# Three chained layers on one core: value products by pairs of query blocks, projections and output products at fixed steps

## The chip, the cores and the metric

The kernel runs on one core of a Trainium2 chip. The metric is the device time of one execution in microseconds (us), as the median of several. TensorE (PE in the profile) multiplies matrices, VectorE (DVE) and ScalarE (ACT) work on vectors and empty PSUM, where products land, GpSimd (POOL) works on vectors in SBUF, and SyncE (SP) issues most transfers. Each engine works through a queue of its own in order; semaphores hold an instruction until what it needs is there.

## The reference, cut to what matters

Three layers follow each other on 4 batches of 544 rows (32 global and 512 local ones) of width 512.

```python
out_l = sm(where(|i - j| <= 32, q k^T / 8) with 32 global keys) v       # 8 heads of 64, local and global rows
x = rows of all heads side by side                                       # [4, 544, 512]

for e in range(4):                                                       # second layer: 4 experts, each one causal head
    q, k, v = x @ wq[e], x @ wk[e], x @ wv[e]
    a = softmax(where(j > i, -1e9, q @ k^T / 8))
    out += gate[e] * (a @ v @ wo[e])                                     # gate: top 2 of 4

xk = mu_k * x + (1 - mu_k) * x_prev                                      # third layer, x_prev: the row before
xr = mu_r * x + (1 - mu_r) * x_prev
result = sigmoid(xr @ w_r) * (relu(xk @ w_k) ** 2 @ w_v)
```

## The kernel before, in words

The text calls the three layers A, C and D. The projections that feed C are called B; they run inside A and C.

**A** (step `n`, the loop at L813) computes local attention for 16 pairs of heads and leaves its result transposed in SBUF, one tile `xT[b]` a batch (channels on partitions, 544 rows along the free dimension). From `n` = 16 to 32 the loop at L861 spreads the 15 projection groups of batch 0 over its steps. The steps of C begin at `n` = 33, while A still ends.

**B** (`b_groups`, L624) is 15 groups a batch, in this order: `b_split` of the first half (256 rows; `xT` into a high and a low part, ACT L385 and POOL L386), value products of blocks 0 and 1 (`b_v`, 12 products each), q and k of the first pair of experts, q and k of the second pair (`b_qk`, 12 products each); then the same for the second half (288 rows), with the gating `b_gate` behind the value products. Every product with a weight is three (`mm3`, L93: high by high, high by low, low by high).

**C** (`c_step(m)`, L759) goes over 36 units, 9 a batch: query blocks 0 to 2 of the first pair of experts, the rows of the last 32 of the batch ("l"), block 3, and blocks 0 to 3 of the second pair. Step `m` holds these parts, in this order of the code:

- the scores of unit `m` (`c_qk`: PE L102, DVE L504, ACT L506);
- the norm of unit `m-1` (`c_norm`: DVE L517 to L519, POOL L522);
- some groups of the list `fill`: of B for batch b+1, and of the output products of batch b-1 (`e_wo`, 8 groups of 6 products, evicted by ACT L622);
- the transposes of unit `m-2` (`c_tp`: PE L531 into PSUM, evictions to the tile `cpt` by ACT L534 for one expert and DVE L536 for the other);
- the value products of unit `m-3` (`c_pv`: PE L602, each block alone; PSUM is emptied into `ytH` and `ytL` by ACT L612 and DVE L613 when block 2 and when block 3 are done);
- at `m` = 32 (`MIX`) the mixing of the first rows for D (`d_mix(0)`: ACT L675 and L679, DVE L676, POOL L680), and at `m` = 33 to 36 the first four products `d_k` of D;
- in two of three steps a job of the list `jobs` (L808): load 128 rows of a weight of D (21 loads, the first of them `wo`), and the split of the load before into high and low parts (`split_wd`, L137: ACT L144, L145, L159, POOL L147, L160, DVE L149, L150, L151, the first of each engine queued behind the engine's last score, norm or A instruction by `after`).

`fill` gets 15 groups when a batch begins and, at its fourth step, the 8 output groups in front of them; the number taken at a step follows from what is left (L774 to L776):

```python
k = -(-len(fill) // max(1, 9 - it)) if not (it < 3 and b > 0) else 2
if it in (3, 4, 5, 6) and b > 0:
    k = max(k, 3)
```

The order of this code is a wish, not the order of the queues. The build (`schedule_with_timeline_sim=True`, L975) plays all instructions through a simulated timeline and queues on each engine what is ready there first, the earlier in the code where two are ready. `after(ins)` (`tc.issue_after`) forbids an instruction to be queued ahead of `ins` on its engine; it makes nothing wait for `ins` to end.

**D** (the loop at L883) takes the 2176 rows in 9 blocks: `d_k`, `d_v` and `d_r` on PE with `d_mix` of the next block beside them.

Buffers that matter here: PSUM tag "a" with 6 tiles (scores, transposes, projections, output products, `d_k`), PSUM tag "x" with 2 (`y` of `c_pv`), `cpt` 2, `x` (the split) 1, `y` 2, `vC` 2, `qk` 3.

Of the kernel before, what the change touches and what calls it, by code (L numbers as in the profile page):

```python
# [18 lines left out]
S = SL + SG  # L19
# [10 lines left out]
MIX, K0, FIRST = 32, 33, 4  # L30
# [15 lines left out]
def chain_kernel(ctx: ExitStack, tc: tile.TileContext, kq, vw, vgd, w_gate, wq, wk, wv, wo,  # L46
# [526 lines left out]
    def l_tp(b):  # L573
        t = pl
        o = T("ptl", [5, 128], f"ptl{b}")
        pT = ps_t(f"lT{b}")
# [10 lines left out]
    yps, yHL = {}, {}  # L587

    def c_pv(b, ep, i):
        if ep == 0 and i == 0:  # L590
            yHL[b] = [T("y", [2, S], f"yt{s}{b}", F32R) for s in "HL"]
        if i in (0, NB - 1):
            yps[b, ep] = ps_x(f"y{b}{ep}{i}")
        yp = yps[b, ep]
        pt = cpt.pop((b, ep, i))
        lastq = i == NB - 1
        n = 160 if lastq else 128
        o0 = 0 if lastq else i * 128
        for j in range(i + 1):
            for e in ((0, 1), (1, 0))[j % 2]:  # L600
                hh = 2 * ep + e
                nc.tensor.matmul(yp[64 * e:64 * e + 64, o0:o0 + n], vC[b][:, j, hh * HD:(hh + 1) * HD],  # L602
                                 pt[:, e, j, 0:n], start=j == 0, stop=j == i and not lastq)
        if lastq:
# [4 lines left out]
        if i >= NB - 2:  # L609
            yH, yL = yHL[b]  # L610
            cc, src = (slice(384, S), yp[:, :160]) if lastq else (slice(0, 384), yp[:, :384])
            nc.scalar.copy(yH[:, ep, cc], src)  # L612
            nc.vector.tensor_sub(yL[:, ep, cc], src, v32(yH[:, ep, cc]))  # L613

    def e_wo(b, c, half):
        yH, yL = yHL[b]
        cc = slice(half * HALF, (half + 1) * HALF)
        p = ps_t(f"po{b}{c}{half}")
        for ep in range(2):
            mm3(p[:, :HALF], woS[0][:, ep, c * 128:(c + 1) * 128], woS[1][:, ep, c * 128:(c + 1) * 128],  # L620
                yH[:, ep, cc], yL[:, ep, cc], ep == 0, ep == 1)
        nc.scalar.copy(xT[b][:, c, 1 + half * HALF:1 + (half + 1) * HALF], p[:, :HALF])  # L622

    def b_groups(b):  # L624
        gs = []
# [11 lines left out]
    def wo_groups(b):  # L637
        return [lambda c=c, half=half: e_wo(b, c, half) for c in range(NC) for half in range(2)]
# [120 lines left out]
    def c_step(m):  # L759
        nonlocal fill, pending  # L760
        if m < NCU:
            b, it = divmod(m, 9)
            u = units[m]
            l_qk(b) if u[1] == "l" else c_qk(*u)
        else:
            b, it = B, m - NCU
        if it == 0 and b + 1 < B:
            fill += b_groups(b + 1)
        if it == 3 and 0 < b:
            fill = wo_groups(b - 1) + fill  # L770
# [3 lines left out]
        k = -(-len(fill) // max(1, 9 - it)) if not (it < 3 and b > 0) else 2  # L774
        if it in (3, 4, 5, 6) and b > 0:
            k = max(k, 3)  # L776
        for g in fill[:k]:
            g()
        del fill[:k]
# [3 lines left out]
        if 0 <= m - 3 < NCU:  # L783
            u = units[m - 3]
            if u[1] != "l":
                c_pv(*u)
# [192 lines left out]
```

## Time and profile before

| | us |
|---|---|
| median of 3 runs | 567.74 (565.76 to 572.1) |
| the profiled execution | 568.83 |
| its span, first to last instruction | 567.0 |
| of it PE busy | 544.6 |

The profiled execution has 1.8 us outside its span. In the rows below an instruction stands as engine, line of the kernel, operation, the tile that it writes <- the tiles that it reads, and its form (partitions times columns); "po" are the output products, "pv" and "pb" the projections, "C" the scores, "cT" the transposes, "y" the value products of C. Time in brackets is idle time of the engine just before, with what ended it. The rows that carry the argument stand below the change.

### The profile page before, as it was taken

What the parts mean: (1) busy time and instruction counts of PE and PEld (TensorE: products, weight loads), DVE (VectorE), ACT (ScalarE), POOL (GpSimd) and SP (SyncE); (2) the same over time, 40 slices, a digit from 0 to 9 for tenths busy, and PEclk for the clock granted to TensorE, in tenths of its full rate; (3) what the DMA queues carried; (4) which work ended last, traced back from release to release, by engine and by line L of the source; (5) the groups of instructions that cost most, each with busy time, mean ns of one, the idle gap of its engine ahead of it and who ended that gap; (6) DMA issues with size and microseconds to landing.
All of it is one profiled execution on the core that took longest, in us unless ns stands there. A gap on an engine that the chain in (4) does not pass through costs nothing.

```text
span 567.0 us, 12852 instructions
## 1 busy us (share of the span) xinstructions
PE 544.6 (96%) x4670; PEld 458.4 (81%) x4670; DVE 326.5 (58%) x1129; ACT 337.0 (59%) x1019; POOL 312.7 (55%) x416
## 2 busy tenths in 40 slices
PE   6899999999898999999987999999999999999997
PEld 3576777788787888788776798989898989898895
DVE  3677765664888779668999656442534252324211
ACT  5789765674667586668688468454545453534221
POOL 3578744453568786959688765443434343335120
PEclk9799999999998999899998999999999999999999
DMA  8998433020143442432740220000000010100000
GB/s 326 278 315 249 162 124 125 3 95 1 39 132 129 136 144 94 150 113 76 297 145 5 76 75 15 25 20 18 21 19 32 7 38 2 39 1 37 1 20 37
DMA packets 24383, 51.31 MB, mean 90 GB/s; under 512 B 10112, under 2 KB 11136, under 8 KB 23680
## 3 DMA queue, kind: packets, MB, share of 16 engines
q1 hardware_dynamic: 23744, 50.08, 26.1%
q8 instruction: 37, 0.61, 0.4%
q10 hardware_dynamic: 576, 0.41, 0.2%
q14 instruction: 26, 0.21, 0.1%
HBM read 39.74 MB, written 10.75 MB: 89 GB/s over the span
## 4 chain that ended last, share of the span: by engine, by line
PE 77%; DVE 13%; ACT 4%; POOL 3%; DMA 2%; issue 1%; SPq 0%; ACTq 0%; DVEq 0%; POOLq 0%
PE v L94 5%; PE v L95 5%; PE v L96 5%; PE k L96 5%; PE k L95 5%; PE k L94 5%; PE S L230 4%; PE y L602 3%; PE r L95 3%; PE r L94 3%; PE r L96 3%; PE x L348 3%; PE pT L280 2%; PE C L102 2%; PE cT L531 2%; PE po L94 2%
## 5 line engine op out<-in xcount | busy, mean ns | idle before, releaser
L696 POOL TENSOR_TENSOR kk<-k2r,kk 128x256 fp32r<-128x256 f32 x64 | 48.5, 761 | 83.6 <-ACT kk L695 83.6
L693 DVE TENSOR_TENSOR k2r<-ksr 128x256 f32<-128x256 f32 x64 | 30.6, 477 | 88.2 <-ACT ksr L692 84.6
L522 POOL TENSOR_TENSOR csm<-csm,crc 128x128 f32<-128x128 f32 (+3 forms) x64 | 52.7, 845 | 28.7 <-DVE crc L519 16.6
L243 ACT ACTIVATE sm<-sm,mn 128x160 f32<-128x160 f32 x128 | 53.4, 418 | 22.1 <-DVE mn L240 21.8
L676 DVE SCALAR_TENSOR_TENSOR mmr<-xT,mu,mtr 128x256 f32<-128x256 f32 (+4 forms) x96 | 53.9, 599 | 16.6 <-POOL m0L L680 5.7
L692 ACT ACTIVATE ksr<-k 128x256 f32<-128x256 f32 x64 | 24.1, 377 | 49.3 <-PE k L96 49.2
L261 POOL TENSOR_TENSOR pn<-sm,rc 128x256 f32<-128x256 f32 x64 | 37.9, 613 | 22.7 <-PE pT L280 14.0
L680 POOL TENSOR_TENSOR m1L<-mmr,m1H 128x256 fp32r<-128x256 f32 (+1 forms) x36 | 26.3, 744 | 42.4 <-ACT m1H L679 38.0
L506 ACT ACTIVATE csm<-csm,cmn 128x128 f32<-128x128 f32 (+3 forms) x64 | 35.8, 561 | 19.8 <-DVE cmn L504 14.3
L675 ACT ACTIVATE mtr<-xT,omu 128x256 f32<-128x256 f32 (+4 forms) x96 | 39.7, 441 | 6.8 <-DVE mmr L676 6.6
L695 ACT CAST kk<-k2r 128x256 fp32r<-128x256 f32 x64 | 25.8, 404 | 27.1 <-DVE k2r L693 25.4
L230 PE MATMUL S<-kq 64*64 64x160 f32 x512 | 33.1, 327 | 5.9 <-DMA kq<-in_kq_dram 3.9
L240 DVE CUSTOM_DVE_ANT_0 sm<-S,band 128x160 f32<-128x160 f32 x128 | 33.9, 316 | 5.4 <-PE S L230 5.0
L602 PE MATMUL y<-cpt,vC 128*64 128x128 f32 (+1 forms) x320 | 31.6, 299 | 2.8 <-ACT cpt L534 2.7
L741 DVE TENSOR_TENSOR o<-v,rt 128x512 f32<-128x512 f32 x17 | 11.6, 686 | 36.4 <-ACT m1H L679 21.8
L504 DVE CUSTOM_DVE_ANT_0 csm<-C,causal 128x128 f32<-128x128 f32 (+3 forms) x64 | 29.7, 483 | 4.7 <-PE C L102 4.5
L230 PEld LDWEIGHTS S<-kq 64*64 64x64 f32 x512 | 20.7, 141 | 13.7 <-DMA kq<-in_kq_dram 3.9
L102 PE MATMUL C<-qk 64*128 64x128 f32 (+3 forms) x192 | 29.2, 359 | 0.1
L602 PEld LDWEIGHTS y<-cpt,vC 128*64 128x64 f32 x320 | 20.1, 138 | 10.6 <-issue 4.1
L679 ACT CAST m1H<-mmr 128x256 fp32r<-128x256 f32 (+1 forms) x36 | 13.4, 391 | 25.5 <-DVE mmr L676 13.1
L386 POOL TENSOR_TENSOR x<-xT,x 128x256 fp32r<-128x256 f32 (+1 forms) x32 | 24.2, 784 | 7.8 <-ACT x L385 4.1
L348 PE MATMUL x<-pt,vw 128*64 128x64 f32 x512 | 28.4, 233 | 0.0
(407 smaller groups left out, 1913.5 us busy)
## 6 DMA issues: line engine op xcount, KB each, us to landing
kq<-in_kq_dram SPq DMA_DIRECT2D x15, 688.0 KB, 5.5
vw<-in_vw_dram SPq DMA_DIRECT2D x16, 512.0 KB, 5.4
out_dram<-o SPq DMA_DIRECT2D x17, 256.0 KB, 2.0
wrawv<-in_moe_w_v_dram SPq DMA_DIRECT2D x8, 512.0 KB, 3.6
wrawk<-in_moe_w_k_dram SPq DMA_DIRECT2D x8, 512.0 KB, 3.6
wrawr<-in_moe_w_r_dram SPq DMA_DIRECT2D x4, 512.0 KB, 3.6
dv0H<-wgv SPq DMA_DIRECT2D x4, 256.0 KB, 2.9
dv0L<-wyv SPq DMA_DIRECT2D x4, 256.0 KB, 2.4
```

The source lines that it names most:

```text
L94: nc.tensor.matmul(o, wH, xH, start=start, stop=False)
L95: nc.tensor.matmul(o, wH, xL, start=False, stop=False)
L96: nc.tensor.matmul(o, wL, xH, start=False, stop=stop)
L102: nc.tensor.matmul(op[0], op[a], op[x], start=n == 0, stop=n == 2)
L230: nc.tensor.matmul(st[h][64 * c:64 * c + 64, i * W:(i + 1) * W], t[rr, 64 * blk:64 * blk + 64], t[rr, KT0 + 96 * blk:KT0 + 96 * blk + W], ...
L243: last_act = nc.scalar.activation(ts[:, h, i], ts[:, h, i], AF.Exp, bias=mn[:, c:c + 1], scale=-1.0, accum_out=su[:, c:c + 1])
L348: nc.tensor.matmul(xs[pp][rr, 64 * blk:64 * blk + 64], w, pt[2 * pp + m // 2][:, 2 * h + m % 2, 64 * c:64 * c + 64], start=blk == 0, stop= ...
L522: last_pool = nc.gpsimd.tensor_tensor(t[:, :w], t[:, :w], rc[:, e:e + 1].to_broadcast([128, w]), op=ALU.mult)
L602: nc.tensor.matmul(yp[64 * e:64 * e + 64, o0:o0 + n], vC[b][:, j, hh * HD:(hh + 1) * HD], pt[:, e, j, 0:n], start=j == 0, stop=j == i and ...
L675: nc.scalar.mul(mt[:, cc], xp, omu[:, kind, c:c + 1])
L676: nc.vector.scalar_tensor_tensor(mm[:, cc], x, mu[:, kind, c:c + 1], mt[:, cc], op0=ALU.mult, op1=ALU.add)
L696: nc.gpsimd.tensor_sub(hl[1], k2, v32(hl[0]))
```

## The change

- **Value products by pairs.** `c_pv` is called for odd blocks only and does blocks 2p and 2p+1 into one PSUM tile. It is emptied into `ytH` and `ytL` after each pair: 256 columns and 288 (before: 384 and 160). In the step it stands behind the norm and ahead of the projections, where before it stood behind the transposes.
- **Output kept apart by halves.** One pair of tiles `yH`, `yL` serves all batches; the output groups take its columns as 256 and 288 (before 272 and 272), and are given out by half.
- **Fixed steps.** The table `STEPS` says at which step of a batch each group runs; `plan_fill` makes the plan. The steps of batch b hold: 1: the first split of b+1, and four output groups (first half) of b-1; 2: values 0; 3: values 1, q; 4: k, one output group (second half); 5: q, k, the second split, one output group; 6: two output groups, values 2; 7: values 3, gating; 8: q, k; 9, which is step 0 of the next batch: the last q, k. Of batch 0, 13 groups stay in A and 2 go to step 0 of C. The first output groups of batch 3 stand at step 37, the second behind the last step.
- **First mixing.** `MIX` goes from 32 to 31, and its ACT and DVE instructions are queued behind the last eviction of `cpt` on their engines. `c_tp` now names its evictions as `last_act` and `last_dve`, so the weight splits of a step are queued behind them too.
- **Jobs** run in three of four steps (before two of three).
- **Last rows.** The 32 last rows of a batch are multiplied over all 128 partitions (before over the batch's own 32); the rest of the tile is zeroed by a POOL memset, one a batch.

```diff
-MIX, K0, FIRST = 32, 33, 4
+MIX, K0, FIRST = 31, 33, 4
...
     def c_tp(b, ep, i):
+        nonlocal last_act, last_dve
...
             if e == 0:
-                nc.scalar.copy(pt[:, e, 0:i + 1, 0:128], src)
+                last_act = nc.scalar.copy(pt[:, e, 0:i + 1, 0:128], src)
             else:
-                nc.vector.tensor_copy(pt[:, e, 0:i + 1, 0:128], src)
+                last_dve = nc.vector.tensor_copy(pt[:, e, 0:i + 1, 0:128], src)
...
         o = T("ptl", [5, 128], f"ptl{b}")
+        nc.gpsimd.memset(o[:, NB], 0.0)
...
+    yHL = []
+
+    def c_pv(b, ep, pr):
+
+        if not yHL:
+            yHL.extend(T("y", [2, S], f"yt{s}", F32R) for s in "HL")
+        yp = ps_x(f"y{b}{ep}{pr}")
+        for i in (2 * pr, 2 * pr + 1):
+            pt = cpt.pop((b, ep, i))
+            n = 160 if i == NB - 1 else 128
+            o0 = 128 * (i % 2)
+            for j in range(i + 1):
+                for e in ((0, 1), (1, 0))[j % 2]:
+                    hh = 2 * ep + e
+                    nc.tensor.matmul(yp[64 * e:64 * e + 64, o0:o0 + n], vC[b][:, j, hh * HD:(hh + 1) * HD],
+                                     pt[:, e, j, 0:n], start=j == 0, stop=j == i and i < NB - 1)
+        if pr == 1:
             for e in range(2):
                 hh = 2 * ep + e
-                nc.tensor.matmul(yp[64 * e:64 * e + 64, 128:160], v_last[SG * b:SG * b + SG, hh * HD:(hh + 1) * HD],
-                                 ptl[b][SG * b:SG * b + SG, NB, hh * 32:(hh + 1) * 32], start=False, stop=True)
...
+                nc.tensor.matmul(yp[64 * e:64 * e + 64, 256:288], v_last[:, hh * HD:(hh + 1) * HD],
+                                 ptl[b][:, NB, hh * 32:(hh + 1) * 32], start=False, stop=True)
+        yH, yL = yHL
+        cc, src = (slice(256, S), yp[:, :288]) if pr else (slice(0, 256), yp[:, :256])
+        nc.scalar.copy(yH[:, ep, cc], src)
+        nc.vector.tensor_sub(yL[:, ep, cc], src, v32(yH[:, ep, cc]))
...
+    STEPS = {1: [(0, 0), (1, 0, 0), (1, 0, 1), (1, 0, 2), (1, 0, 3)], 2: [(0, 1)], 3: [(0, 2), (0, 3)],
+             4: [(0, 4), (1, 1, 0)], 5: [(0, 5), (0, 6), (0, 7), (1, 1, 1)], 6: [(1, 1, 2), (1, 1, 3), (0, 8)],
+             7: [(0, 9), (0, 10)], 8: [(0, 11), (0, 12)], 9: [(0, 13), (0, 14)]}
...
+        gs = b_groups(0)
+        plan[0] = gs[13:]
...
+                    if op[0] == 0 and nxt:
+                        plan.setdefault(9 * b + it, []).append(nxt[op[1]])
+                    if op[0] == 1 and wos:
+                        plan.setdefault(9 * b + it, []).append(wos[op[1]][op[2]])
+        plan[9 * B + 1] = wo_groups(B - 1, 0)
+        return gs[:13], plan
...
+        if 0 <= m - 3 < NCU:
+            u = units[m - 3]
+            if u[1] != "l" and u[2] % 2:
+                c_pv(u[0], u[1], u[2] // 2)
+        for g in plan.get(m, []):
             g()
-        del fill[:k]
         if 0 <= m - 2 < NCU:
             u = units[m - 2]
             l_tp(u[0]) if u[1] == "l" else c_tp(*u)
-        if 0 <= m - 3 < NCU:
-            u = units[m - 3]
-            if u[1] != "l":
-                c_pv(*u)
         if m == MIX:
             d_begin()
-            d_mix(0)
+            with after(last_act), after(last_dve):
+                d_mix(0)
...
-        if jobs and m >= J0 and (m - J0) % 3 < 2:
+        if jobs and m >= J0 and (m - J0) % 4 < 3:
             pending.append(jobs.pop(0)())
```

## Rows read from the trace of the kernel before

**Rows 1.** The page's first part: busy time of PE over the span, its share, and the number of instructions.

```profile
PE   544.6 (96%) x4670; PEld 458.4 (81%) x4670; DVE 326.5 (58%) x1129; ACT 337.0 (59%) x1019; POOL 312.7 (55%) x416
```

**Rows 2.** The view of busy time by stretch: A, the four batches of C (one a row), and D. Columns: stretch, its length, busy us (instructions) of each engine, granted clock of TensorE, DMA share, GB/s.

```profile
0.00:126.00 126.00, 118.91 (x1709) 87.84 (x1710) 80.30 (x454) 89.03 (x335) 71.87 (x129) 0.97 0.57 186
...
129.00:178.00 49.00, 45.71 (x434) 39.46 (x434) 34.81 (x142) 31.02 (x92) 28.32 (x32) 0.96 0.20 66
178.00:228.00 50.00, 48.24 (x373) 40.51 (x371) 40.30 (x125) 34.12 (x94) 38.98 (x43) 0.97 0.40 128
228.00:277.00 49.00, 48.90 (x385) 42.03 (x385) 37.38 (x119) 33.07 (x95) 37.77 (x40) 0.97 0.39 132
277.00:327.00 50.00, 43.53 (x361) 36.02 (x359) 41.83 (x112) 37.06 (x103) 40.51 (x44) 0.97 0.32 114
...
327.00:566.00 239.00, 236.36 (x1395) 209.73 (x1392) 89.67 (x172) 111.13 (x302) 94.09 (x128) 1.00 0.07 24
```

**Rows 3.** The view of waits, of PE from 140 to 330 us, three of its four largest: who waited <- for whom, us in total, times, longest.

```profile
PE po L94 <- DVE cpt L536: 3.6, 1, 3.6
PE y L602 <- ACT cpt L534: 2.7, 2, 1.3
...
PE k L94 <- DVE cmn L504: 1.2, 1, 1.2
```

**Rows 4.** The timeline of PE around four of the longest waits of the steps of C, and the first and last of twelve products before the first of them. Columns: start, us, instruction, count, and in brackets the idle time before it.

```profile
171.50 0.40 PE L94 MATMUL pb11k<-x,wk 128*128 128x288 f32 x1
...
173.07 0.29 PE L96 MATMUL pb11k<-x,wk 128*128 128x288 f32 x1
...
176.00 0.66 PE L602 MATMUL y<-cpt,vC 128*64 128x128 f32 x8 [1.34 <-ACT cpt L534]
176.88 0.39 PE L94 MATMUL pv<-wv,x 128*128 128x260 f32 x1 [0.23 <-ACT x L385]
...
228.10 0.39 PE L94 MATMUL pv<-wv,x 128*128 128x260 f32 x1 [1.87 <-ACT x L385]
...
278.19 0.52 PE L531 MATMUL cT<-ident,csm 128*128 128x128 f32 x3 [0.98 <-DVE cpt L536]
...
299.92 0.49 PE L94 MATMUL po<-ytH,woH 128*128 128x272 f32 x1 [3.60 <-DVE cpt L536]
```

**Rows 5.** The timelines of ACT and DVE ahead of the evictions that PE waited for: ACT at 175 and 227 us, DVE from 295 us.

```profile
174.94 0.75 ACT L144 ACTIVATE wgv<-wrawv,tcol 128x512 f32<-128x512 f32 x1
175.59 0.36 ACT L534 COPY cpt<-cT 128x256 f32<-128x256 f32 x1
...
227.65 1.02 ACT L385 CAST x<-xT 128x256 fp32r<-128x256 f32 x3
...
295.60 0.95 DVE L149 TENSOR_SCALAR wyk<-wyk 128x512 uint32<-128x512 uint32 x1 [0.27 <-POOL wyk L147]
296.58 1.10 DVE L151 SCALAR_TENSOR_TENSOR wyk<-wyk,wgk 128x512 uint32<-128x512 uint32 x1
297.60 1.31 DVE L676 SCALAR_TENSOR_TENSOR mmr<-xT,mu,mtr 128x256 f32<-128x256 f32 x1
298.84 0.57 DVE L517 TENSOR_SCALAR crc<-csu 128x2 f32<-128x2 f32 x1
299.32 0.55 DVE L536 COPY cpt<-cT 128x384 f32<-128x384 f32 x1
```

**Rows 6.** The view of busy time by stretch again, of the four stretches of C in which TensorE had the lower clock.

```profile
153.28:156.70 3.42, 3.42 (x18) 3.42 (x18) 2.40 (x8) 1.82 (x4) 2.73 (x4) 0.50 0.03 7
177.18:180.59 3.41, 3.41 (x18) 2.85 (x18) 2.71 (x9) 2.23 (x8) 3.41 (x5) 0.50 0.45 127
228.38:231.79 3.41, 3.41 (x19) 2.63 (x18) 1.49 (x6) 2.57 (x11) 3.41 (x4) 0.50 0.63 211
300.06:303.47 3.41, 3.41 (x16) 3.41 (x17) 3.38 (x10) 2.69 (x9) 2.37 (x3) 0.50 0.02 5
```

**Rows 7.** The timeline of PE: twelve output products (the first of them and what follows the last) from 291 us, and the row that follows twelve of the same from 299.92 us.

```profile
291.11 0.39 PE L94 MATMUL po<-ytH,woH 128*128 128x272 f32 x1
...
292.81 0.43 PE L602 MATMUL y<-cpt,vC 128*64 128x128 f32 x2
...
302.70 0.63 PE L578 MATMUL lT<-ident,pl 128*128 128x128 f32 x2
```

**Rows 8.** The page's part on DMA issues: KB each, median us from issue to landing.

```profile
wrawv<-in_moe_w_v_dram SPq DMA_DIRECT2D x8, 512.0 KB, 3.6
```

**Rows 9.** Groups of instructions by line: busy us, mean ns of one | idle time before. The third row is from the view of one line (ns of the shortest, the median and the longest, first and last start).

```profile
L607 PE MATMUL y<-ptl,vl 32*64 32x32 f32 x32 | 2.4, 228 | 0.0
L354 PE MATMUL xg<-plg,vw 128*64 128x32 f32 x160 | 10.6, 214 | 0.0
L199 POOL MEMSET plg<- x1: 205/205/205, 0.7 to 0.7; 128x128 f32 x1
```

**Rows 10.** The view of one line, DVE L150 (the second step of a weight's split); then the timelines of DVE and POOL at 290 us.

```profile
L150 DVE SCALAR_TENSOR_TENSOR wgv<-wrawv,wgv x8: 679/692/1099, 155.1 to 206.9; 128x512 uint32<-128x512 uint32 x8
L150 DVE SCALAR_TENSOR_TENSOR wgk<-wrawk,wgk x8: 691/836/1782, 254.4 to 306.8; 128x512 uint32<-128x512 uint32 x8
...
289.99 1.78 DVE L150 SCALAR_TENSOR_TENSOR wgk<-wrawk,wgk 128x512 uint32<-128x512 uint32 x1
...
289.94 1.28 POOL L160 TENSOR_TENSOR wk1L<-wyk,wk1H 128x512 fp32r<-128x512 f32 x1 [1.35 <-ACT wk1H L159]
```

More of the change, by code (lines that the diff above doesn't have):

```diff
@@ L585, in l_tp @@
         ptl[b] = o
[L587 to L604, printed above, removed]
+    yHL = []
@@ L605, in c_pv @@
             for e in range(2):
                 hh = 2 * ep + e
-                nc.tensor.matmul(yp[64 * e:64 * e + 64, 128:160], v_last[SG * b:SG * b + SG, hh * HD:(hh + 1) * HD],
-                                 ptl[b][SG * b:SG * b + SG, NB, hh * 32:(hh + 1) * 32], start=False, stop=True)
[L609 to L613, printed above, removed]
+                nc.tensor.matmul(yp[64 * e:64 * e + 64, 256:288], v_last[:, hh * HD:(hh + 1) * HD],
+                                 ptl[b][:, NB, hh * 32:(hh + 1) * 32], start=False, stop=True)
@@ L615, in e_wo @@
+        yH, yL = yHL
+        cc, src = (slice(256, S), yp[:, :288]) if pr else (slice(0, 256), yp[:, :256])
+        nc.scalar.copy(yH[:, ep, cc], src)
+        nc.vector.tensor_sub(yL[:, ep, cc], src, v32(yH[:, ep, cc]))
     def e_wo(b, c, half):
-        yH, yL = yHL[b]
-        cc = slice(half * HALF, (half + 1) * HALF)
+        yH, yL = yHL
+        t0, n = HS[half]
+        cc = slice(t0, t0 + n)
         p = ps_t(f"po{b}{c}{half}")
         for ep in range(2):
-            mm3(p[:, :HALF], woS[0][:, ep, c * 128:(c + 1) * 128], woS[1][:, ep, c * 128:(c + 1) * 128],
+            mm3(p[:, :n], woS[0][:, ep, c * 128:(c + 1) * 128], woS[1][:, ep, c * 128:(c + 1) * 128],
@@ L621, in e_wo @@
                 yH[:, ep, cc], yL[:, ep, cc], ep == 0, ep == 1)
-        nc.scalar.copy(xT[b][:, c, 1 + half * HALF:1 + (half + 1) * HALF], p[:, :HALF])
+        nc.scalar.copy(xT[b][:, c, 1 + t0:1 + t0 + n], p[:, :n])
     def b_groups(b):
@@ L635, in b_groups, with wo_groups, plan_fill @@
         return gs
-    def wo_groups(b):
-        return [lambda c=c, half=half: e_wo(b, c, half) for c in range(NC) for half in range(2)]
+    def wo_groups(b, half):
+        return [lambda c=c: e_wo(b, c, half) for c in range(NC)]
+    STEPS = {1: [(0, 0), (1, 0, 0), (1, 0, 1), (1, 0, 2), (1, 0, 3)], 2: [(0, 1)], 3: [(0, 2), (0, 3)],
+             4: [(0, 4), (1, 1, 0)], 5: [(0, 5), (0, 6), (0, 7), (1, 1, 1)], 6: [(1, 1, 2), (1, 1, 3), (0, 8)],
+             7: [(0, 9), (0, 10)], 8: [(0, 11), (0, 12)], 9: [(0, 13), (0, 14)]}
+    def plan_fill():
+        plan = {}
+        gs = b_groups(0)
+        plan[0] = gs[13:]
+        for b in range(B):
+            nxt = b_groups(b + 1) if b + 1 < B else None
+            wos = [wo_groups(b - 1, half) for half in range(2)] if b > 0 else None
+            for it, ops in STEPS.items():
+                for op in ops:
+                    if op[0] == 0 and nxt:
[4 more added lines that the diff above has]
+        return gs[:13], plan
     tokens = [(u * NU_D, NU_D) for u in range(8)]
@@ L759, in c_step @@
     def c_step(m):
-        nonlocal fill, pending
+        nonlocal pending
         if m < NCU:
-            b, it = divmod(m, 9)
             u = units[m]
[L764 to L770, printed above, removed]
+            l_qk(u[0]) if u[1] == "l" else c_qk(*u)
         if 0 <= m - 1 < NCU:
@@ L773, in c_step @@
             l_norm(u[0]) if u[1] == "l" else c_norm(*u)
[L774 to L777, printed above, removed]
+        if 0 <= m - 3 < NCU:
[3 more added lines that the diff above has]
+        for g in plan.get(m, []):
             g()
-        del fill[:k]
         if 0 <= m - 2 < NCU:
@@ L803, in c_step @@
             fetch_wd("v", 1, "L")
-    fill = b_groups(0)
+    fill, plan = plan_fill()
     NFILL = len(fill)
@@ L877, in chain_kernel @@
         c_step(m)
-    for g in wo_groups(B - 1):
+    for g in wo_groups(B - 1, 1):
         g()
```

## The prediction, made before the changed kernel was run

> **What bounds the kernel now.** I read the page's first part, then busy time by stretch, then PE's waits, then the timelines at the longest of them. PE is busy for 544.6 of 567.0 us [rows 1]. By stretch [rows 2] the reader should compare PE with its stretch: D has 236.4 of 239.0 us with idle time only at its end, so D can't be shortened by this change, and every microsecond that C ends sooner comes off the time. A, up to 126 us, has 118.9 us, and the change takes nothing out of it but two groups of projections. C, from 129 to 327 us, has 186.4 of 198.0 us in its four rows, 43.5 of 50.0 in the last batch. Its lower granted clock (0.96 or 0.97) is the second loss. So the place to look at is what PE waited for in C [rows 3], and where.
>
> Three of the four longest places in the timeline [rows 4] are the beginnings of batches: 176.0, 228.1 and 278.2 us. At the first of them the last projection ended at 173.4 us, and after one unit of scores PE had only things left whose inputs ACT or DVE still had to make: value products, the first projection of the batch after next (which needs the split of `xT`), a transpose that needs a PSUM tile emptied. PE sat 1.34 + 0.23, 1.87 and 0.98 us. The fourth, 3.60 us at 299.9 us, is another kind: an output product wanted a PSUM tile that DVE had still to empty.
>
> What made these evictions late is in the queues ahead of them [rows 5]. On ACT a weight's split (L144, 0.75 us) stands before the eviction at 175.6 us; before 228 us three of the copies of `b_split` (1.02 us) do. On DVE, before 299.3 us, there are L149 and L151 of a split and L676 of the first mixing, 0.95 + 1.10 + 1.31 us, and a norm of 0.57 us: 3.9 us of DVE work in a row ahead of the eviction.
>
> **Second loss: the clock.** TensorE's granted clock fell to 0.50 (1.2 instead of 2.4 GHz) four times in C, for 3.41 us each, and each fall follows one of PE's longer waits: the first of the two for `cpt` on ACT and those at 176, 228 and 300 us [rows 3, 4, 6]; the waits of 0.98 us at 278 us and of 1.2 us for L504 have none behind them. Twelve output products took from 291.11 to 292.81 us at the full clock, 1.70 us, and from 299.92 to 302.70 us at half, 2.78 us [rows 4, 7]. So 39% of such a stretch is lost, 1.33 us a fall.
>
> **The change, part by part.**
>
> *Fixed steps.* The number of projections and output products stays 15 and 8 groups a batch; their order to the buffers changes. What counts is what PE has at a batch's beginning. Step 9 now holds the last q and k of the second half, 24 products. Twelve such took from 171.50 to about 173.2 us; the last starts at 173.07 us [rows 4], so two groups are some 3.5 us of PE work, more than any of the three waits there. Step 1 adds four output groups, 24 products, 3.4 us at the pace of [rows 7], while ACT and POOL make the split, whose first user is now a step later. That covers both kinds of wait: I take off all of 1.34 + 0.23 + 1.87 + 0.98 = 4.42 us. What it costs: the other steps get less. By counts, a step of batches 1 and 2 now carries 12 to 30 products beside scores, transposes and value products; steps 2 and 7 have 12 alone. There the unit's own work (block pairs of value products at steps 2 and 7) fills in, so I price them at nothing. Without that cover a step would wait about as at 278 us, 1 us.
>
> *A's last groups.* Two groups of batch 0 go from the end of A to step 0: their PE work is moved by a few us and not changed, price zero; PE is dense on both sides.
>
> *First mixing and splits queued behind evictions, mixing a step earlier, jobs in three of four steps.* The 21st job moves from step 31 to step 27 (job k at 1 + 3(k//2) + k%2, now 1 + 4(k//3) + k%3). The splits that stood on DVE up to 313 us end a few steps earlier, and none may be queued ahead of the eviction of its step. This takes L149, L151 and L676 from before the eviction at 299.3 us: minus 3.60 us, and I also take the 1.2 us for L504 [rows 3], a score's reduction that was late on DVE in the same crowd. What is late next is the mixing itself: its rows are needed by `d_k` a step or two later, and one step of lead was added. The loads stay 21, 512 KB each and 3.6 us to landing [rows 8], issued a few steps earlier on SP, and the stores of the split parts with them; what they could collide with, the fetches for D, stays at steps 33 and 35, behind them.
>
> *Clock.* Three of the four falls follow waits that go: 3 x 1.33 = 4.0 us.
>
> *Value products by pairs, halves.* The number of products and of evictions stays (two a pair of experts and batch, of 256 and 288 columns for 384 and 160), so no instruction is saved. But a new neighbourhood arises: the value products of an odd block stand right behind the scores of the next step, and need the eviction that was queued at the end of the step before. There are 16 such pairs. Where it is late, PE waits as in the two rows for `cpt` on ACT, 2.7 us in two [rows 3], 1.35 us each. Ends: nothing (a dense PE puts projections in between) and 16 x 1.35 = 21.6 us. The even block's own products, ready a step longer, lie ahead, so I take two of 16: plus 2.7 us.
>
> *Last rows on 128 partitions.* 32 PE instructions take 2.4 us on 32 partitions, 75 ns each; the nearest wide ones, 128 partitions by 64 and 32 columns, 10.6 us for 160, 66 ns each [rows 9]. Price zero; nothing excludes a gain or loss of 0.3 us. The memset is 205 ns [rows 9], four in all; POOL has 49.5 us a batch and uses some 36 [rows 2], so it hides; 0.8 us if not.
>
> **Sum.** 4.42 + 3.60 + 1.2 + 4.0 = 13.2 us off, 2.7 us on: minus 10.5 us. The span would be 556.5 us. The profiled execution had 568.83 us, 1.1 over the median, so I take the difference from the median: 567.74 - 10.5 = 557.2 us.
>
> **The rivals.** *All of it goes.* The rest of C's waits (the first, 1.3 us, of the two on `cpt`, its fall of 1.33 us, and small ones) go as well and no pair waits: 16 us off, 551 to 552 us. For it: with fixed steps no step is without PE work. Against: that first wait for `cpt` stands at no beginning of a batch, and nothing in the change queues `b_split` behind an eviction.
>
> *DVE and POOL become the bound.* The splits don't vanish; they move from the last batch, where DVE is busy 41.8 of 50 us, into batches 1 and 2 with 40.3 of 50 and 37.4 of 49 [rows 2]. An L150 took 0.69 us in the median of the first eight, but 1.78 us at 290 us, where it began with a POOL subtraction of 1.28 us running, and 0.84 us in the median of the last eight [rows 10]. With denser splits more of them meet POOL. If each of the batches 1 and 2 then gets one wait like that of 3.60 us with its fall, 2 x 4.9 = 9.8 us of the 10.5 come back: 567 us. The Trainium skill has a rule for this, SBUF — State Buffer, section "Who interferes with whom": a VectorE instruction with two SBUF inputs and a GpSimd instruction that reads SBUF share a port pair, and the later one is blocked for the whole of the earlier. The 1.78 us row agrees with it (0.69 us behind an instruction of 1.28 us); the median of 0.69 says that most splits of the earlier batches missed each other. Against this rival: evictions now go ahead of splits, so a long split delays mostly the next split.
>
> *The pairs wait.* If most of the 16 pairs find their odd block's eviction unfinished, each costs 1.35 us: all of them 21.6 us against 13.2 us off, 567.74 + 8.4 = 576 us. From 10 of 16 on the kernel is slower than before. For it: the two rows on `cpt` are exactly this wait, behind one unit of scores. Against: in both PE had run out of projections, and the eviction now stands ahead of the splits that had delayed it.
>
> *The queueing changes nothing:* the eviction waits for its transposes, and those for POOL's norm; if DVE was idle rather than crowded there, 3.60 us would stay. DVE shows no gap between L149 and the eviction [rows 5], so I give this no case of its own.
>
> **How the numbers follow.** The forecast, 557.2 us (its own range 553.5 to 562), has 0.50. All goes (551.5): 0.20. DVE and POOL (567, or 562 to 567 where one batch is hit): 0.18. The pairs (570 to 576): 0.12. A measurement of this kernel can tell about 1% from no change, 5.7 us. Faster by more than that, under 562.1: 0.50 + 0.20, and nearly nothing of the third, 0.70. Slower, over 573.4 us: most of the pairs, 0.10. The rest, 0.20, is the same. The range goes from 549.5 (all goes, less 2 us for the spread of the runs shown) to 568 us, which leaves out the pairs and a little at the low end.
>
> **What would show it.** Right: at the three beginnings of batches q and k products stand where PE waited; no fall of the clock behind them; DVE evicts `cpt` before splits and mixing in the last batch, and C takes some 187 us from its first score to D's first `d_v`. Wrong: PE rows of `y` behind scores with a wait for `cpt` in brackets, ten or more; or waits of 2 to 4 us in batches 1 and 2 with DVE rows over 1 us ahead of an eviction. D's 239 us must stay; if D changes, the argument that only C counts is wrong.

## The result, and the profile after

| | kernel before | changed kernel |
|---|---|---|
| median of 20 runs each, us | 567.36 (563.77 to 573.4) | 572.89 (569.27 to 576.96) |
| ratio, 95% interval | 1 | 1.0104 (1.008 to 1.0129) |
| profiled execution, its span, us | 568.83, 567.0 | 569.27, 567.5 |

The change makes the kernel 1% slower, where 557.2 us (549.5 to 568) was predicted. The profiled execution is the quickest of the twenty, so it may show less waiting than the others have.

The page's first part, for [rows 1]:

```profile
PE 544.7 (96%) x4670; PEld 458.4 (81%) x4670; DVE 337.9 (60%) x1129; ACT 337.8 (60%) x1019; POOL 312.7 (55%) x420
```

As many DVE instructions as before take 11.4 us more. The view of busy time by stretch, for [rows 2], the four batches of C and D:

```profile
129.00:178.00 49.00, 45.68 (x435) 39.30 (x432) 39.26 (x141) 30.36 (x90) 33.07 (x36) 1.00 0.25 80
178.00:228.00 50.00, 47.14 (x374) 40.95 (x372) 43.04 (x126) 35.80 (x99) 37.56 (x42) 0.97 0.42 135
228.00:277.00 49.00, 46.01 (x375) 39.73 (x373) 44.88 (x123) 34.54 (x97) 42.95 (x45) 1.00 0.40 129
277.00:327.00 50.00, 49.47 (x382) 40.09 (x383) 36.14 (x110) 34.69 (x100) 31.33 (x39) 1.00 0.26 96
327.00:566.00 239.00, 235.67 (x1392) 208.61 (x1391) 90.36 (x172) 111.30 (x301) 94.70 (x128) 1.00 0.06 24
```

DVE, the third pair, is at 43.0 and 44.9 us in batches 1 and 2 (40.3 and 37.4 before) and at 36.1 in the last (41.8). PE got 6 us more into the last batch and 4 us less into the two before it. The waits of PE from 100 to 365 us, the longest four, for [rows 3]:

```profile
PE y L603 <- ACT cpt L535: 5.6, 3, 2.6
PE pb21q L94 <- DVE qk L406: 2.1, 1, 2.1
PE v L94 <- ACT kk L719: 1.1, 1, 1.1
PE pT L280 <- DVE mn L240: 1.1, 1, 1.1
```

Of [rows 3] the 3.6 us for DVE's eviction in the last batch and the 1.2 us of L504 are gone; the wait for `cpt` on ACT has doubled, and three others are new. The timeline of PE at these, and what it did ahead of the first in C, for [rows 4]:

```profile
119.32 0.63 PE L280 MATMUL pT<-ident,pn 128*128 128x128 f32 x4 [1.07 <-DVE mn L240]
...
170.20 0.30 PE L96 MATMUL pb10k<-x,wk 128*128 128x288 f32 x1
...
170.87 0.55 PE L102 MATMUL C<-qk 64*128 64x128 f32 x6
171.34 0.43 PE L603 MATMUL y<-cpt,vC 128*64 128x128 f32 x2
174.40 0.43 PE L603 MATMUL y<-cpt,vC 128*64 128x128 f32 x2 [2.62 <-ACT cpt L535]
174.76 0.40 PE L94 MATMUL pb11q<-x,wq 128*128 128x288 f32 x1
...
203.09 0.38 PE L94 MATMUL pb21q<-x,wq 128*128 128x256 f32 x1 [2.07 <-DVE qk L406]
...
277.14 0.43 PE L603 MATMUL y<-cpt,vC 128*64 128x128 f32 x2 [2.64 <-ACT cpt L535]
...
358.72 0.50 PE L94 MATMUL v<-wv0H,kk 128*128 128x512 f32 x1 [1.14 <-ACT kk L719]
```

Products of q and k (`pb10k`) now stand just ahead of the batch's beginning, and batch 1 begins at 170.9 us instead of 174.1 (first score of each). Then the even block's value products run, and the odd block's wait 2.6 us for their eviction on ACT. The last q and k of the half (`pb11q`) come only behind these, as the change puts value products ahead of projections in a step. Why the eviction is late is on the queues. ACT, DVE and POOL from 168 us, for [rows 5]:

```profile
172.62 0.22 ACT L446 ACTIVATE gd<-gd 128x16 f32<-128x16 f32 x1 [2.64 <-DVE gd L445]
172.74 0.74 ACT L144 ACTIVATE wgv<-wrawv,tcol 128x512 f32<-128x512 f32 x1
173.39 0.39 ACT L405 CAST qk<-pb10q 128x288 fp32r<-128x288 f32 x1
173.66 0.41 ACT L405 CAST qk<-pb10k 128x288 fp32r<-128x288 f32 x1
173.95 0.39 ACT L535 COPY cpt<-cT 128x256 f32<-128x256 f32 x1
...
169.66 0.21 DVE L435 TENSOR_TENSOR gt<-lg 128x64 f32<-128x64 f32 x1
169.79 0.85 DVE L436 TENSOR_TENSOR eq<-lg 128x64 f32<-128x64 f32 x1
170.56 0.16 DVE L443 TENSOR_REDUCE m<-lg 128x4 f32<-128x16 f32 x1
170.67 0.96 DVE L437 TENSOR_TENSOR eq<-eq,tri 128x64 f32<-128x64 f32 x1
171.56 1.02 DVE L445 TENSOR_TENSOR gd<-lg,m 128x16 f32<-128x16 f32 x1
...
168.37 4.18 POOL L522 TENSOR_TENSOR csm<-csm,crc 128x384 f32<-128x384 f32 x4
```

L446 is the exponential of `b_gate`, the gating of the next batch. It is 0.22 us of work, and ACT sits 2.64 us in front of it, with the eviction (L535) four places behind. It waits for L445, the last of three two-input instructions on 16 to 64 elements a partition (L436, L437, L445) that take 0.85, 0.96 and 1.02 us while POOL's four norms run. The view of one line, L446 (idle time of ACT before it, us, times), in the changed kernel and then in the kernel before:

```profile
  DVE gd L445: 9.8, 4
```

```profile
  DVE gd L445: 1.4, 2
```

Of the 9.8 us, 2.61 are in A, where the gating of batch 0 runs, and 2.64, 0.40 and 4.10 in C. The wait of 2.07 us at 203 us is another kind: ahead of the L406 that PE waits for stand two long instructions of a split on DVE, L149 (1.13 us) and this one:

```profile
200.81 1.63 DVE L151 SCALAR_TENSOR_TENSOR wyv<-wyv,wgv 128x512 uint32<-128x512 uint32 x1
```

### The profile page after: what moved, and what is told of

It reads as the page before. It is cut to its first block, busy times and chain, and to the rows that moved or that the text cites. A ratio compares the mean times of both kernels' runs of the same rounds, so it can differ in the third digit from the quotient of the medians.

```text
span 567.5 us, 12858 instructions
## 1 busy us (share of the span) xinstructions
PE 544.7 (96%) x4670; PEld 458.4 (81%) x4670; DVE 337.9 (60%) x1129; ACT 337.8 (60%) x1019; POOL 312.7 (55%) x420
## 4 chain that ended last, share of the span: by engine, by line
PE 75%; DVE 12%; ACT 5%; issue 3%; POOL 3%; DMA 2%; ACTq 0%; POOLq 0%; SPq 0%; DVEq 0%
PE k L95 5%; PE k L94 5%; PE k L96 5%; PE v L94 5%; PE v L95 5%; PE v L96 5%; PE S L230 5%; PE x L348 3%; PE y L603 3%; PE pT L280 3%; PE C L102 2%; PE r L96 2%; PE r L94 2%; PE r L95 2%; PE cT L532 2%
## 5 line engine op out<-in xcount | busy, mean ns | idle before, releaser
L522 POOL TENSOR_TENSOR csm<-csm,crc 128x128 f32<-128x128 f32 (+3 forms) x64 | 49.9, 800 | 22.0 <-DVE crc L519 17.5
L261 POOL TENSOR_TENSOR pn<-sm,rc 128x256 f32<-128x256 f32 x64 | 38.0, 614 | 32.6 <-PE pT L280 18.9
L230 PE MATMUL S<-kq 64*64 64x160 f32 x512 | 34.7, 330 | 5.9 <-DMA kq<-in_kq_dram 4.7
L603 PE MATMUL y<-cpt,vC 128*64 128x128 f32 (+1 forms) x320 | 34.0, 297 | 5.6 <-ACT cpt L535 5.6
L240 DVE CUSTOM_DVE_ANT_0 sm<-S,band 128x160 f32<-128x160 f32 x128 | 34.1, 316 | 7.1 <-PE S L230 6.1
L765 DVE TENSOR_TENSOR o<-v,rt 128x512 f32<-128x512 f32 x17 | 11.6, 686 | 34.2 <-ACT m1H L703 21.8
L504 DVE CUSTOM_DVE_ANT_0 csm<-C,causal 128x128 f32<-128x128 f32 (+3 forms) x64 | 29.3, 481 | 2.9 <-PE C L102 2.7
L348 PEld LDWEIGHTS x<-pt,vw 128*64 128x64 f32 x512 | 24.6, 139 | 4.7 <-issue 3.4
L94 PE MATMUL v<-wv0H,kk 128*128 128x512 f32 x68 | 26.9, 396 | 1.1 <-ACT kk L719 1.1
```

What stands on the lines that cost most here:

```text
L94: nc.tensor.matmul(o, wH, xH, start=start, stop=False)
L230: nc.tensor.matmul(st[h][64 * c:64 * c + 64, i * W:(i + 1) * W], t[rr, 64 * blk:64 * blk + 64], t[rr, KT0 + 96 * blk:KT0 + 96 * blk + W], ...
L348: nc.tensor.matmul(xs[pp][rr, 64 * blk:64 * blk + 64], w, pt[2 * pp + m // 2][:, 2 * h + m % 2, 64 * c:64 * c + 64], start=blk == 0, stop= ...
L522: last_pool = nc.gpsimd.tensor_tensor(t[:, :w], t[:, :w], rc[:, e:e + 1].to_broadcast([128, w]), op=ALU.mult)
```

## Experiments

All are five rounds against the kernel before on the same chip; the ratio is to that kernel, with its 95% interval. The chip is not the same in all of them, and the intervals reach some 0.0035 to either side, so two ratios are clear of each other from about 0.005 on.

**The changed kernel again.** No edit.

> The changed kernel unaltered, to see another execution of it beside the kernel before on the same chip. All theories expect a ratio of 1.010. Of its profile the gating theory (the gate's Exp on ACT stands in the queue ahead of evictions and waits for DVE) expects two waits of PE of 2 to 3 us for cpt behind idle time of ACT before L446; the density theory (splits in three of four steps stretch DVE against POOL) expects DVE busy for some 10 us more in C than in the kernel before, and waits spread over batches 1 and 2.

572.5 us, 1.0081 (1.0045 to 1.0116). Same waits: 6.0 us in 3 for `cpt` on ACT, 2.1 us for L406. Here the clock fell to half twice in C, at 176 and 206 us, right behind the waits that ended at 174.9 and 205.2 us.

**Is it the gating's place?** Two ways. First, only a step later in the table:

```diff
-             7: [(0, 9), (0, 10)], 8: [(0, 11), (0, 12)], ...
+             7: [(0, 9)], 8: [(0, 10), (0, 11), (0, 12)], ...
```

> The changed kernel with the gating one step later (step 8 ahead of q and k, where step 7 held it behind the value product that it needs). Gating theory: the two waits of 2.6 us for cpt go, 4 to 6 us off, ratio 1.000 to 1.003 against the kernel before. Density theory: the waits only change place, ratio 1.008 to 1.012. Pairs theory (value products right behind the scores wait wherever the chain is late): 1.006 to 1.012, with other waits of y for cpt.

572.0 us, 1.0066 (1.0027 to 1.0106), waits of 5.9 us in 3. This decides nothing: in the built queue L446 still stands ahead of the same eviction. Then out of the table, behind the transposes of step 8, and queued behind their evictions:

```diff
         if 0 <= m - 2 < NCU:
             ...
             l_tp(u[0]) if u[1] == "l" else c_tp(*u)
+        if m % 9 == 8 and m // 9 + 1 < B:
+            with after(last_act), after(last_dve):
+                b_gate(m // 9 + 1)
```

> The changed kernel with the gating taken out of step 7, put behind the transposes of step 8 and queued behind their evictions on ACT and DVE (moving it in the table alone had left ACT's queue as it was, with the gate's Exp one place range ahead of the eviction). Gating theory: both waits of 2.6 us for cpt go, 4 to 6 us off the changed kernel, ratio 0.997 to 1.002 against the kernel before. Density theory: under 2 us off, as the next DVE row in line is late too, ratio 1.005 to 1.010.

566.5 us, **0.9996 (0.996 to 1.0032)**. The waits of value products for ACT are gone. PE's waits from 140 to 365 us, the longest:

```profile
PE po L94 <- DVE qk L406: 1.9, 1, 1.9
PE po L94 <- DVE ql L414: 1.2, 1, 1.2
PE v L94 <- ACT kk L719: 1.2, 1, 1.2
PE pb21q L94 <- DVE qk L406: 1.1, 1, 1.1
```

So the gating's place is 0.0085 of the time, 4.8 us, against the repeated run: nearly the whole loss against the kernel before, but not the gain of 10.5 us that was forecast.

**Is it the pairs?** Each block's value products by themselves behind the transposes, in the changed kernel and with the gating mended:

```diff
-            if u[1] != "l" and u[2] % 2:
-                c_pv(u[0], u[1], u[2] // 2)
...
+            if u[1] != "l":      # behind c_tp; evicted at the odd block
+                c_pv(*u)
```

> The changed kernel with the value products of each block alone and behind the transposes of its step, as in the kernel before (halves, fixed steps, jobs and queueing as changed). Pairs theory: the waits of y for cpt (5.6 to 6.0 us in three) go and 4 us or more come off, ratio 1.000 to 1.003. Gating and density theory: late evictions are waited for at another place, under 2 us off, 1.005 to 1.012.

> The changed kernel with the gating queued behind the evictions of step 8 and with each block's value products by themselves behind the transposes, as before the change. Theory (the pairs only show a lateness that the gating causes): without the gating's lateness the pairs cost nothing in C, so 0.9985 to 1.001, as with the gating alone (0.9996). Rival (the pairs cost by themselves): single blocks alone took 0.0029 off the changed kernel and would take it off here too: 0.9967, with the waits of value products for evictions (0.8 us in the run of the gating alone) gone and the last value products some 1 us earlier.

570.15 us, 1.0052 (1.002 to 1.0084), and 568.64 us, 1.0031 (0.9998 to 1.0065). In the first the value products wait no more, and projections stand there instead:

```profile
PE pb11q L94 <- ACT cpt L535: 3.6, 1, 3.6
PE pb21q L94 <- ACT cpt L535: 1.6, 1, 1.6
PE pb31q L94 <- DVE cpt L537: 1.6, 1, 1.6
```

The first of these stands at the beginning of batch 1, where ACT sits idle for 3.23 us ahead of L446 and evicts `cpt` behind it. The late eviction is the cause, and the pairs only the place where it shows. With the gating mended, single blocks gain nothing; 1.0031 is if anything worse than 0.9996.

**Is it the density of the splits on DVE?** Jobs in two of three steps again in the changed kernel; dense only up to step 9; three of four in the kernel before; two of three with the gating mended:

```diff
-        if jobs and m >= J0 and (m - J0) % 4 < 3:
+        if jobs and m >= J0 and (m - J0) % 3 < 2:              # e3, e10
+        if jobs and m >= J0 and (m < 10 or (m - J0) % 3 < 2):  # e9
```

> The changed kernel with the jobs (loads and splits of D's weights) in two of three steps again. Density theory: DVE busy time in C falls back by 6 to 10 us and the time by about 5 us, ratio 1.000 to 1.003. Gating theory: still 1.007 to 1.012, and the waits of 2.6 us stand. In both the last batch gets the last splits back on DVE, which may cost 1 to 3 us there.

> The changed kernel with a job in every step up to step 9 and then in two of three, so that the last job comes at about the same step (27) as in the changed kernel, but batches 1 and 2 have no more splits a step than the kernel before. Density theory: batches 1 and 2 as with two of three (start of batch 3 near 272 us, four before the kernel before) and the last batch as in the changed kernel: ratio 0.992 to 0.998. Gating theory: the waits of 2.6 us stay, 1.004 to 1.010.

> The kernel before with one part of the change alone, the jobs in three of four steps. Density theory: DVE busy for 6 to 10 us more in C, ratio 1.005 to 1.015 unless the emptier last batch pays it back. Gating theory: no loss, and the 3.6 us wait of the last batch shrinks, ratio 0.990 to 1.000.

> The changed kernel with the gating behind the transposes of step 8, queued behind their evictions (as in the run of the gating alone, 0.9996 of the time before), and also the weights' splits at two of three steps. Theory: the two losses are separate, the gating's in the batches with a next one, the crowding of DVE by three splits in four steps in batches 1 and 2. The two of three alone took 0.0026 off the changed kernel, so both give 0.997, with the last batch again slower (a wait for an eviction on DVE at about 300 us). Rival, one cause: the denser splits hurt only because they stretched the gate's chain on DVE; with the gating gone from there they cost nothing, and two of three only puts splits back into the last batch: 1.000 to 1.004.

In the order of the four: 572.08 us, 1.0055 (1.0012 to 1.0097); 572.3 us, 1.0076 (1.0042 to 1.0111); 570.63 us, 1.0057 (1.0021 to 1.0093); 567.78 us, 1.0018 (0.9987 to 1.0049). In the first, batch 3 begins at 272.4 us, 3.4 us ahead of the repeated run, and the last batch gives it back. PE and then DVE there:

```profile
303.72 0.80 PE L102 MATMUL C<-qk 64*128 64x384 f32 x6 [1.96 <-DVE cpt L537]
```

```profile
300.94 1.64 DVE L150 SCALAR_TENSOR_TENSOR wgk<-wrawk,wgk 128x512 uint32<-128x512 uint32 x1
302.50 0.56 DVE L519 TENSOR_TENSOR crc<-crc,gate 128x2 f32<-128x2 f32 x1
302.99 0.68 DVE L537 COPY cpt<-cT 128x512 f32<-128x512 f32 x1
```

It is the pattern of [rows 5, 10], a long split ahead of an eviction in the last batch. Denser jobs take this wait out of the last batch (in the kernel before, 3.6 us became 0.6) and bring others earlier, 3.3 us for a copy of `x`. In the kernel before they cost 0.6% by themselves, as the density theory forecast; the gating theory forecast no loss there and missed. In the changed kernel undoing them brings 0.0026, and with the gating mended it costs 0.0022, neither clear of noise. So density has a cost of its own, but it is not what the gating's place repairs, and the gain of 3.60 us that I booked for moving the splits is not a gain of the whole.

**Queueing, without holding splits back.** Evictions keep their own names, so that only the mixing is queued behind them:

```diff
-                last_act = nc.scalar.copy(pt[:, e, 0:i + 1, 0:128], src)
+                evs["act"] = nc.scalar.copy(pt[:, e, 0:i + 1, 0:128], src)
```

> The changed kernel in which the transposes' evictions no longer hold back the weight splits (only the first mixing stays queued behind them). If holding splits back is what makes them meet POOL and delay the chain of the next unit: ratio 1.000 to 1.004. Gating and density theory: no gain, 1.008 to 1.02, as evictions can stand behind splits again.

573.75 us, 1.0099 (1.0063 to 1.0134): no help, 4.1 us in 3 for `cpt` on ACT, and `po` 2.1 us for L406.

**All three undone.** Gating queued, single blocks, two of three:

> All three undone together: gating queued behind the evictions of step 8, single blocks, splits at two of three steps. What is left of the change are the fixed steps, the halves, the mixing a step earlier and queued. If the three costs are separate (0.0085, 0.0029 and 0.0026 of the time before), 1.0081 less 0.014 gives 0.994. If they are one lateness seen in three ways, no more than the gating alone gives: 0.9985 to 1.001.

571.25 us, 1.0058 (1.0018 to 1.0098). The three are not separate costs that add up; both forecasts missed.

**The first mixing at its old step, not queued,** with the gating mended; and the same a second time:

```diff
-MIX, K0, FIRST = 31, 33, 4
+MIX, K0, FIRST = 32, 33, 4
...
-            with after(last_act), after(last_dve):
-                d_mix(0)
+            d_mix(0)
```

> The changed kernel with the gating queued behind the evictions of step 8, and the first mixing at step 32 again and not queued behind evictions. Theory (the end of C and the start of D are late because the second half of the first mixing needs a buffer that the last value products hold, and the earlier mixing gives nothing): no difference from the gating alone, 0.9985 to 1.001, and the wait of 1.2 us of the first d_v for kk stays. Rival (the mixing at step 31 takes ACT and DVE from the last evictions, which delays the last pair of value products): the last value products end 1 to 2 us earlier, D starts earlier, 0.997 to 0.998.

> The kernel with the gating queued behind evictions and the mixing at step 32 again, a second time, for comparison on the same chip: 0.997 as before (0.994 to 1.000), d_v waits 1.0 us for kk.

565.94 us, 0.997 (0.994 to 1.0), and 565.5 us, 0.9965 (0.993 to 1.0): 0.003 better than with the gating alone, with intervals that overlap. The mixing's early step gave nothing, and may cost 1.5 us.

**What holds D up?** From the first product of `r` to the end the kernel before takes 222.5 us, the changed one 223.9. PE has no wait in this stretch in the kernel before, and one in the changed kernel, the 1.14 us for `kk`. My theory was a chain from the last value products, which free `vC`, through the mixing. It goes into the free buffers of `raw` instead: with the two edits above, in the kernel before, and in the changed kernel.

```diff
-                tag = "y" if kind == 0 else ("vC", "cpt")[n % 2]
+                tag = "y" if kind == 0 else ("vC", "cpt")[n % 2] if n else "raw"
```

> The kernel with the gating queued behind evictions and the mixing at step 32 again, and the second half of the first mixing goes into the two buffers of raw (free since the last weight was split) instead of vC, which the last value products hold. Theory (a chain from the last value products through this mixing sets the end): the wait of 1.0 us of the first d_v for kk goes and the first mixing is done some 5 us earlier, D takes 222.5 us from the first r instead of 223.7: 1.0 to 1.5 us less than the same kernel without it (e17_again), about 0.994 of the time before. Rival (ACT and DVE have that much to do anyway, and the mixing only moves ahead of the last evictions of C): the d_v wait goes, but waits of 1 us or more come up ahead of 330 us; no difference from e17_again.

> The kernel before with the second half of the first mixing in the buffers of raw. There the first d_v of the second block finds its kk just in time (no wait). Theory: the chain is not longer than TensorE's own work there, so 0.999 to 1.001, with kk some us earlier than its product. Rival (mixing earlier crowds DVE in the last batch): 1.003 or more, with a longer wait than 3.6 us at 300 us.

> The changed kernel with that one edit alone, the gating left where it was. Theory: 1.0 to 1.5 us off (0.002 to 0.003), from 1.008 to 1.0104 to some 1.006 to 1.008; the 2.6 us waits of value products stay. Rival: no difference, 1.008 or more.

566.86 us, 0.9998 (0.9962 to 1.0034); 572.42 us, 1.0106 (1.0062 to 1.015); 572.2 us, 1.0111 (1.0076 to 1.0146). The theory falls: in the first the wait for `kk` stays (1.4 us), D takes 224.2 us, and nothing is gained. In the kernel before the earlier mixing costs 1%: the waits of value products for `cpt` on ACT go from 2.7 us in 2 to 4.0 in 3, which is 1.3 us of it; the rest is not shown. So 1.14 of D's 1.4 us are PE's wait for `kk`, and why `kk` is late stays open.

**A's last two groups of projections, back in A,** in the kernel with gating and mixing mended, and in the changed kernel:

```diff
-        plan[0] = gs[13:]
+        plan[0] = gs[15:]
...
-        return gs[:13], plan
+        return gs[:15], plan
```

> The kernel with the gating queued behind evictions and the mixing at step 32 again (0.9965 and 0.997 of the time before), and the last two groups of projections of batch 0 back in A, as before the change. Theory (they covered a wait in A): the wait of 1.1 us at about 119 us goes, C begins some 2.3 us later and is 3.4 us shorter, 1.1 us less in all: about 0.9945 to 0.995. Rival (A has other waits that come up instead, and C's first steps then lack PE work): 0.997 or more, with a new wait between 129 and 160 us.

> The changed kernel with that one edit alone. Theory: 1.1 us off (0.002), 1.006 to 1.0085 of the time before, the wait of 1.1 us at 119 us gone. Rival: 1.008 to 1.0104 as without it.

563.28 us, **0.9923 (0.9886 to 0.9959)**, and 572.14 us, 1.0067 (1.0027 to 1.0107). The first is the best kernel here, quicker than the one before by 0.4 to 1.1%. Its waits from 100 to 365 us and its batches 2 and 3:

```profile
PE po L94 <- DVE qk L406: 1.7, 1, 1.7
PE po L94 <- DVE ql L414: 1.6, 1, 1.6
PE lT L580 <- POOL pl L572: 1.3, 1, 1.3
PE pb21q L94 <- DVE qk L406: 1.0, 1, 1.0
PE v L94 <- ACT kk L719: 1.0, 1, 1.0
```

```profile
228.00:277.00 49.00, 48.02 (x385) 41.26 (x385) 43.18 (x127) 36.55 (x101) 41.61 (x44) 1.00 0.39 128
277.00:327.00 50.00, 47.51 (x387) 39.88 (x388) 35.01 (x108) 32.88 (x94) 30.32 (x39) 1.00 0.21 78
```

The wait of 1.07 us at 119 us is gone, and the granted clock is 1.00 in all of C. From the first score to the first product of `r` C takes 207.3 us (130.2 to 337.6), where the kernel before has 215.2 (129.4 to 344.6); the four falls of the clock that it no longer has are 5.3 us of that at the prediction's 1.33 us each.

But the edit does two things at once. With thirteen groups spread over A's steps instead of fifteen, the gating of batch 0 also runs later: its exponential stands at 118.47 us, not at 109.70. On DVE its chain is directly ahead of L240, the reduction of scores that PE waited for at 119 us. In the changed kernel, and then in the kernel before:

```profile
116.23 1.12 DVE L436 TENSOR_TENSOR eq<-lg 128x64 f32<-128x64 f32 x1
...
117.38 0.54 DVE L437 TENSOR_TENSOR eq<-eq,tri 128x64 f32<-128x64 f32 x1
117.84 0.60 DVE L445 TENSOR_TENSOR gd<-lg,m 128x16 f32<-128x16 f32 x1
118.36 0.31 DVE L240 CUSTOM_DVE_ANT_0 sm<-S,band 128x160 f32<-128x160 f32 x1
```

```profile
109.10 0.22 DVE L436 TENSOR_TENSOR eq<-lg 128x64 f32<-128x64 f32 x1
...
109.35 0.23 DVE L437 TENSOR_TENSOR eq<-eq,tri 128x64 f32<-128x64 f32 x1
109.50 0.17 DVE L445 TENSOR_TENSOR gd<-lg,m 128x16 f32<-128x16 f32 x1
```

The three take 2.26 us instead of 0.62, 1.64 us more ahead of L240, which is more than PE's wait of 1.07 us. In the kernel before POOL is idle until 109.76 us; in the changed one L323 and then two L261 run beside the chain (1.13 and 1.18 us). With the groups back the three take 0.61 us again. So the rows speak for the gating here too and not for missing cover; no run separates the two.

## Why the prediction was wrong

**Which step failed.** In *fixed steps* the sum counted PE's products: "the other steps get less", "so I price them at nothing", 1 us without cover. But a step moves all that it issues, and step 7 also moves `b_gate`. It stands directly behind the value projection that it needs, as before the change, but in another step; there its exponential got ahead of the odd block's eviction on ACT, and its inputs come from a chain on DVE that POOL's norms stretch. Idle time in front of it went from 1.4 to 9.8 us, 7.1 of it in C. Putting it behind the evictions of step 8, and nothing else, brings 0.0085, shown by experiment. That is 4.8 of the some 16 us between forecast and measurement; the rest is taken term by term below, read from the runs and only in part tested. It was in the diff: `b_groups` has the gating as its eleventh group, `STEPS` puts it at step 7, and [rows 5] showed ACT's queue as the place where evictions are late.

**The three waits at the beginnings** (4.42 us). The 1.87 us at 228 us went. At the other two PE waits longer than before, 2.62 and 2.64 us, for the odd block's eviction. The last q and k, which were to cover this, stand behind the waiting value products; with single blocks they stand ahead of them and wait for the same eviction themselves, 3.6 us. Batches 1 and 3 do begin earlier, at 170.9 and 273.6 us instead of 174.1 and 276.7, but batch 2 at 225.5 instead of 225.7. From its first score to D's first `d_v` C takes 195.6 us, not 187 (199.7 before).

**The pairs** (two of 16, 2.7 us): three waits, 5.6 us, two of them long. The count came out, by luck, as two was picked between 0 and 16 without a row for it; the size did not, 2.6 us for 1.35, and the gating makes that size. By themselves they cost nothing that these runs show.

**The 3.60 and 1.2 us of the last batch** went, and the last batch gained, but not the whole: the splits' long instructions delay other evictions earlier. That half of the rival *DVE and POOL become the bound* was right: DVE is 11.4 us busier, PE waits 2.07 us in batch 1 behind a long split with a fall of the clock after it, and denser jobs alone cost the kernel before 0.6%. But the profile shows one such wait and not the two of its price, and less density did not mend the changed kernel, while the gating's queue place did.

**The clock** (4.0 us). In place of four falls in C the profiled execution has one, at 203.8 us behind the wait that ended at 203.09, and the repeated run has two. Each run lists span and mean granted clock. In 19 runs of the kernel before, those beside the last row of the table, they lie along a line of 3.9 us for 0.01 of clock (3.3 to 4.8 in the sets beside the other experiments), so the forecast stood for 0.010 more.

| runs | mean span, us | mean clock | kernel before beside it |
|---|---|---|---|
| changed kernel again | 570.7 | 0.9856 | 565.9, 0.9839 |
| gating queued | 564.9 | 0.9938 | 565.5, 0.9846 |
| gating, mixing | 563.6 | 0.9912 | 565.9, 0.9852 |
| gating, mixing, A's groups | 561.9 | 0.9912 | 566.2, 0.9812 |

The changed kernel got 0.002. With the gating mended it is 0.009, with the mixing too 0.006, with A's groups back 0.010: the 4.0 us were there. But of the 5.8 us between the first two rows some 3.2 go with the clock by that line, and of the last row's 4.3 us 3.9 do, which leaves 0.4 us for all the rest (by the other lines, from 1.0 to less than nothing). Of the gain in waits, 9.2 less 2.7 us in my sum, a part came: PE's idle time in the four rows of C falls from 11.6 to 9.7 us, and to 7.6 in the best kernel. New waits stand there (`po` for L406 and L414, 3.3 us in the best kernel), and D gives some back. This is read from the runs and not tested by itself.

**A's two groups** (priced zero, "PE is dense on both sides"). Zero was too little: without them the gating of batch 0 comes later, and PE waits 1.07 us at 119 us. Putting them back takes the mended kernel from 0.9965 to 0.9923, and its mean span from 563.6 to 561.9 us at the same mean clock, where 1.1 us was expected; in the changed kernel it gives 0.001 to 0.004. These differences are not clear of noise, and whether cover or gating makes them is not shown; the rows at 116 us speak for the gating.

**D's 239 us "must stay".** From its first product of `r` on, D grew by 1.4 us, and by 1.2 to 1.7 us in every kernel here with the new C. All but some 0.3 us of it is PE's wait for `kk` (0.9 to 1.4 us), which the kernel before does not have. So the argument that only C counts was wrong by about that much, and why `kk` is late is open.

## What to carry to other kernels

When a step is moved, write down what it puts on each queue, and for every small instruction that ends up ahead of an eviction ask what it waits for: 0.22 us of work held an engine 2.64 us. Price a wait that is removed by what the engine does next, not by its length: here two of three waits came back longer, until the cause behind them was queued out of the way. And work that is taken out of one place shifts whatever was spread out beside it: two groups fewer in A moved the gating there by some 9 us, to where GpSimd was at work.

## What the hardware showed

Two-input VectorE instructions on 16 to 64 elements a partition took 0.85, 0.96 and 1.02 us behind GpSimd norms that took 4.18 us for four; L445 took 0.16 to 0.17 us in the kernel before and up to 1.03 in the changed one. They ended at 170.64, 171.63 and 172.58 us, and the last three norms at 170.56, 171.56 and 172.56. This agrees with the Trainium skill, SBUF — State Buffer, section "Who interferes with whom": a VectorE instruction with two SBUF inputs contends with a GpSimd instruction that reads SBUF, and the one that comes later is blocked for the whole of the other. Not expected was what this does to a chain of tiny instructions. In these rows their size plays no part, each waits out one norm, and L445 is stretched sixfold. Two others of the chain, L435 and L438, began at 169.66 and 172.51 us, just ahead of the next GpSimd instruction, and took 0.21 us.

Most of what separates two runs of one and the same kernel goes with the mean granted clock: over 19 runs of the kernel before it went from 0.973 to 0.991, and the span with it at 3.9 us for 0.01 (correlation -0.86); four other sets of its runs give 3.3 to 4.8 us.
